# Attention, soft experts and feed-forward on one core: a fixed order for the feed-forward part, two more slots for weight loads, and longer rows in two kinds of loads

## The chip, the cores and the metric

The kernel runs on one core of one Trainium2 chip. The metric is the device time of one launch in microseconds (us). Three runs of the kernel before took 878.2, 876.0 and 877.66 us (median 877.66).

## What is computed

Three parts follow one another on 2304 tokens (4 batches of 576, 8 heads of 64):

```python
scores = scale * q @ k^T                              # per batch and head, 576x576
kth    = np.partition(scores, -32)[..., -32]          # keep the 32 largest of a row
attn   = softmax(where(scores >= kth, scores, -1e9)) @ v
x      = attn as [2304, 512]

logits = x @ phi                                      # [2304, 32]: 8 experts x 4 slots
slot_input = softmax(logits, axis=0).T @ x
slot_out[e] = relu(slot_input[e] @ w1[e]) @ w2[e]     # w1 512x1024, w2 1024x512
x      = softmax(logits, axis=1) @ slot_out           # the mix back to tokens

h      = x @ w_in                                     # 512x2048, float64
g      = where(h >= 1, h, where(h <= -1, 0, (h + 1)**2 / 4))
out    = g @ w_out                                    # 2048x512, float64
```

## The kernel before

**Attention** takes 16 head pairs through an order written by hand: the table `ORDER` names small operations, and each entry's letter says how many frames (one per pair) behind it runs. Among the entries are `c0` to `c6`: the conversion of one 128x512 tile of `w_in` from float64 to float32 by bit operations (`narrow`, L213 to L225: absolute value of the high word, maximum, low word scaled by 2^-51, shift by 3, integer add, sign, product with the sign), 16 tiles in all, stored to the DRAM tiles `cv_d` and loaded again later.

**Weight loads** all go through one queue on SP. `wload` (L135) takes the next entry of `worder`, a free 512 KB slot from `wfree`, and starts the transfer; a slot returns to `wfree` when the tile pool that owned it is done. The order is: `w1` (32 tiles), `w2` (32 tiles, w_32 to w_63), converted `w_in` and raw float64 `w_out` (16 tiles). `w2` and `cv_d` come in runs of 2 KB, `w_out` in runs of 4 KB.

**Experts.** For each of two groups of four experts: h = slot_input @ w1 (L804), so = relu(h) @ w2 (L823, four experts packed in row strips), a copy of it on ACT (L828) and a transpose (L831, copied by DVE at L835). Meanwhile `mix` turns the logits into the token-mix matrix `cT` (transposes L790 into one of the two PSUM buffers of the pool `ps_m`, copied out by ACT at L792). `m_first` (L841) multiplies slot_out with the first 512 columns of `w_in`; `m_rest` (L850) does the other 1536; `m_spread` (L865) unpacks one of them. So h of the feed-forward part is cT with m, and needs no 512-deep product.

**Feed-forward.** Tokens are cut into 6 blocks t of 384, the 2048 inner columns into 16 chunks f of 128: 96 steps (t, f). The list `steps` takes blocks 0 and 1 together, f by f (32 steps), then blocks 2 to 5 one after the other (64 steps). A step issues `emit_g` for the step two later: h (L898), two activations (L900, L901), then on DVE the clip (L902), a copy to the rounded high part gh (L904) and the rest gl (L905); then `emit_o` (L916): nine matmuls, 3 row tiles by gh·wh, gh·wl, gl·wh. In the first 32 steps each chunk of `w_out` is also made ready by `wo_prep`: the seven operations of `narrow`, on ACT (L213, L215, L217), POOL (L219 maximum, L223 integer add, L225 product with the sign) and DVE (L221 shift), then the high part wh on ACT (L891) and the low part wl on DVE (L892). In a step's name below, (t, f) is block and chunk.

In this part the order of the instructions on each engine is made by the scheduler, from the program order and its cost estimates. The last `NLAST` = 3 steps run row tile by row tile, so that each result row can be copied out (L920) and stored (L921).

Of the kernel before, what the change touches and what calls it, by code (L numbers as in the profile page):

```python
# [7 lines left out]
ET = mybir.EngineType  # L8
# [11 lines left out]
P = 128  # L20
# [20 lines left out]
NEG = -1.0e30  # L41
CW = 512
# [3 lines left out]
NRAW = 2  # L46
# [19 lines left out]
z3a H0b G31a S40a c0b T30b M21a c1b K11a L3a E40b T31b mc B0a P00a O21a mc c3b R3b C40a  # L66
# [7 lines left out]
def kernel_body(tc, qT, kT, vP, phi, w1, w2, w_in, w_out, out, fast, flag):  # L74
# [8 lines left out]
    cT = cpool.tile([P, NT], F32R, name="cT")  # L83
# [21 lines left out]
    cv_d = [p_dram.tile([P, CW], F32, name=f"cv_d{i}") for i in range(NCV)]  # L105
# [10 lines left out]
    worder += [(2, 0, 0), (2, 0, 1)] + [(3, 0, n) for n in range(NWE // 2)] + [(4, 0, NWE + n) for n in range(NRAW)] + [(2, 0, n) for n in range(2, 2 * NHP)]  # L116
# [14 lines left out]
    wfree = list(slots_a)  # L131
# [9 lines left out]
    def wload(n):  # L141
        while n > 0 and wfree and wnext[0] < len(worder):
            l, e, c = key = worder[wnext[0]]
            slot = next((x for x in wfree if l < 4 or len(x) == 1), None)
            if slot is None:
                return
            wfree.remove(slot)
            ring.append(slot)
            full, parts = slot_tiles(slot, f"w_{wnext[0]}", I32 if l == 4 else F32)
            if l == 0:  # L150
                src = w1[e, c * P:(c + 1) * P, :].rearrange("p (n f) -> p n f", n=2)
            elif l == 1:
                src = w2[e, c * 2 * P:(c + 1) * 2 * P, :].rearrange("(n p) f -> p n f", p=P)
            elif l == 4:
                src = w_out[c * P:(c + 1) * P, :].bitcast(I32).rearrange("p (n f) -> p n f", n=2)
            else:
                src = None
            if full is not None and src is not None:
                dmas = [(full, src)]
            elif src is not None:  # L160
                dmas = [(parts[m], src[:, m, :]) for m in range(2)]
            else:
                n0, c0 = divmod(c, 2)
                at = [NC1 * (2 * c0 + m) + n0 if l == 2 else NHP * NC1 + 2 * c + m for m in range(2)]
                dmas = [(parts[m], cv_d[at[m]]) for m in range(2)]
# [482 lines left out]
    def emit(name, pi):  # L648
        k = name[0]
        if k == "l":  # L650
            op_late(pi, name[1])
        elif k == "z":
            op_split(pi + 1, int(name[1]))
        elif k == "m":
            if pi % NHP == NHP - 1:
                op_moe(pi, k)
        elif k in "cd":
            if k == "c" or pi < NWE:
                i = pi + min(pi, NWE) + (k == "d")
                if i < NCV:  # L660
                    conv_op(i, int(name[1]))
        else:
# [51 lines left out]
    wfree.extend(cv_slots + half_slots)  # L714
# [41 lines left out]

    def mix():
        wide = [P, NR + 1, B, NSLOT]
# [20 lines left out]
        for b in range(B):  # L779
# [6 lines left out]
            for rows in (range(NR), (NR,)):  # L786
# [5 lines left out]
                nc.scalar.copy(cT[:, b * S + rows[0] * P:b * S + rows[0] * P + w],  # L792
# [6 lines left out]
    for g in range(2):  # L799
# [46 lines left out]
    def m_rest():  # L846
# [7 lines left out]
        for n in range(1, NC1):  # L854
            rows = slice(32 * n, 32 * n + 32)
# [27 lines left out]
    def wo_prep(f):  # L883
        if f < NWE:
            wo = wtile[(3, 0, f // 2)][f % 2]
        else:
            tr = p_t.tile([P, 2, CW], I32, name="tr_l", tag="h1s", bufs=2)
            sg = p_t.tile([P, CW], BF16, name="sg_l", tag="sg_l", bufs=1)
            wo = narrow(wtile[(4, 0, f)], tr, sg, range(7))
        wh, wl = slot_tiles(w_slots[f], "whl", F32R)[1]  # L890
        nc.scalar.copy(wh, wo)  # L891
        nc.vector.tensor_tensor(wl, wo, wh.bitcast(F32), op=ALU.subtract)  # L892
        wo_t[f] = (wh, wl)

    def emit_g(s_):
# [27 lines left out]
    m_first()  # L923
    for k in range(CLA):
        wo_prep(k)
    for s_ in steps[:GA]:
        emit_g(s_)
    for i, s_ in enumerate(steps[:-NLAST]):
        t, f = s_
        if i == 1:  # L930
            mhl = m_rest()
        if t == 1 and f % 4 == 1 and f // 4 < NC1 - 1:
            m_spread(f // 4 + 1, *mhl)
        if t == 0 and f + CLA < NF:
            wo_prep(f + CLA)
        if i + GA < len(steps):
            emit_g(steps[i + GA])
        emit_o(t, f, range(NS))
    for s_ in steps[GA - NLAST:] if NLAST > GA else []:
        emit_g(s_)  # L940
    for n in range(NS):
        for s_ in steps[-NLAST:]:
            emit_o(*s_, [n])
# [65 lines left out]
```

## Time and profile before

| | us |
|---|---|
| median of three runs | 877.66 |
| span of the profiled execution | 872.0 |
| its TensorE busy time | 821.5 (94%) |
| its VectorE / ScalarE / GpSimd busy time | 685.8 / 644.8 / 485.4 |
| last expert matmuls end, first o matmuls start | 614.71, 634.20 |
| last o matmul of the blocks 0 and 1, last of all | about 720, 865 |

The page gives the busy time of each engine, the busy tenths in 40 slices of 21.8 us, and the chain of work that ended last. Line numbers are those of the kernel before unless the text says otherwise. The profiled execution's span, 872.0 us, is 5.7 us below the median of the runs, which also hold what lies around the span; sums are made in the span's time and then moved by that 5.7 us.

### The profile page before, as it was taken

The page shows a single profiled execution, that of the slowest core. Times are in us where ns is not written, and L with a number is a line of the kernel's source. Part 1 is how long each engine was busy: PE and PEld are TensorE (multiplying, and loading weights), DVE is VectorE, ACT ScalarE, POOL GpSimd, SP SyncE. Part 2 cuts the span into 40 slices and gives each one's busy share as a digit, 9 for nine tenths or more (in the row PEclk, how much of TensorE's full clock was granted, in tenths as well). Part 3 has the DMA queues.
Part 4 walks back from the last instruction along what each step waited for, and adds up shares of the span by engine and source line. Part 5 has one row for each costly group of instructions (what it writes and reads, how often), then busy time and mean ns, then how long its engine had stood idle before and what let it go on. Part 6 is the DMA issues. An engine that isn't in the chain of part 4 may idle for free.

```text
span 872.0 us, 17711 instructions
## 1 busy us (share of the span) xinstructions
PE 821.5 (94%) x5695; PEld 674.7 (77%) x5695; DVE 685.8 (79%) x3084; ACT 644.8 (74%) x1292; POOL 485.4 (56%) x494
## 2 busy tenths in 40 slices
PE   4889999999999999999999999799698899999996
PEld 3678989988989988988988988632266678888885
DVE  6999999988999989999989994103389995666663
ACT  5688999988998988998988987412578766545453
POOL 2577888877888877888877774100467740000000
PEclk9799999999999999999999999899799999999999
DMA  8453563553353353353452536699940001001001
GB/s 240 124 152 96 165 176 98 156 157 89 103 142 92 112 133 89 102 142 87 117 134 78 157 101 205 206 343 386 399 175 1 0 2 73 37 0 38 1 37 40
DMA packets 49461, 108.59 MB, mean 125 GB/s; under 512 B 8304, under 2 KB 8304, under 8 KB 49360
## 3 DMA queue, kind: packets, MB, share of 16 engines
q1 hardware_dynamic: 49040, 106.73, 40.2%
q8 instruction: 47, 0.77, 0.4%
q10 hardware_dynamic: 320, 0.66, 0.3%
q14 instruction: 54, 0.44, 0.2%
HBM read 70.70 MB, written 8.91 MB: 91 GB/s over the span
## 4 chain that ended last, share of the span: by engine, by line
PE 78%; DVE 10%; DMA 6%; ACT 3%; POOL 1%; issue 1%; ACTq 0%; POOLq 0%; SPq 0%; DVEq 0%
PE s_ps L311 20%; PE o_ps L916 17%; PE av_ps L485 14%; PE pt_ps L457 7%; PE s_ps L413 4%; PE av_ps L486 3%; PE rem_ps L230 3%; DMA w<-in_moe_w_dram 2%; DMA w<-in_moe_w_out_dram 2%; PE h L804 2%; DVE cand L338 2%; PE moe_ps L569 2%; DMA w<-cv_d 1%; PE h_ps L898 1%; PE xT_ps L534 1%
## 5 line engine op out<-in xcount | busy, mean ns | idle before, releaser
L311 PE MATMUL s_ps<-kh,q 128*128 128x288 f32 x640 | 208.1, 342 | 16.4 <-DVE q L266 9.0
L916 PE MATMUL o_ps<-whl,ghl 128*128 128x512 f32 x864 | 216.9, 395 | 5.0 <-DVE ghl L904 4.0
L916 PEld LDWEIGHTS o_ps<-whl,ghl 128*128 128x128 f32 x864 | 159.1, 188 | 44.7 <-DVE ghl L904 7.1
L445 POOL TENSOR_TENSOR ssb<-ssb,pen 128x576 f32<-128x576 f32 x141 | 180.4, 1284 | 18.3 <-ACT pen L442 15.8
L311 PE MATMUL s_ps<-kl,q 128*128 128x288 f32 x640 | 181.2, 299 | 0.0
L338 DVE MAX8 cand<-ssb 128x8 f32<-128x82 f32 (+1 forms) x1008 | 164.2, 228 | 5.0 <-ACT ssb L329 4.0
L311 PEld LDWEIGHTS s_ps<-kh,q 128*128 128x128 f32 x640 | 123.6, 193 | 34.7 <-DVE q L266 9.4
L485 PE MATMUL av_ps<-v_sb,ptb 128*128 128x65 f32 (+1 forms) x1280 | 147.1, 261 | 0.4 <-ACT xT L547 0.4
L485 PEld LDWEIGHTS av_ps<-v_sb,ptb 128*128 128x128 f32 (+1 forms) x1280 | 141.1, 181 | 5.2 <-issue 2.6
L311 PEld LDWEIGHTS s_ps<-kl,q 128*128 128x128 f32 x640 | 124.4, 194 | 0.3
L422 DVE MAX8 l<-s_ps 128x8 f32<-128x576 f32 x144 | 109.2, 758 | 18.3 <-PE s_ps L413 17.9
L442 ACT ACTIVATE pen<-ssb,kb 128x576 bf16<-128x576 f32 x141 | 110.3, 792 | 4.5 <-POOL kb L438 3.3
L329 ACT COPY ssb<-s_ps 128x576 f32<-128x576 f32 x144 | 91.1, 641 | 25.3 <-PE s_ps L311 21.8
L448 ACT ACTIVATE ssb<-ssb,nm 128x576 f32<-128x576 f32 x141 | 109.0, 785 | 0.6 <-POOL ssb L445 0.6
L900 ACT ACTIVATE rg<-h_ps,half 128x384 f32<-128x384 f32 x96 | 55.2, 579 | 71.0 <-PE h_ps L898 70.8
L396 POOL TENSOR_SCALAR mb<-ssb,top 128x576 bf16<-128x576 f32 x48 | 83.3, 1736 | 19.2 <-DVE top L345 9.2
L902 DVE SCALAR_TENSOR_TENSOR rg<-h_ps,rg 128x384 f32<-128x384 f32 x96 | 52.9, 554 | 47.4 <-ACT rg L901 47.1
L467 ACT COPY ptb<-pt_ps 128x512 f32<-128x512 f32 x144 | 82.4, 598 | 3.3 <-PE av_ps L485 3.3
L457 PE MATMUL pt_ps<-ident,ssb 128*128 128x128 f32 x576 | 84.3, 273 | 0.2
L398 DVE TENSOR_SCALAR_CACHE_REDUCE mb<-ssb,top 128x576 bf16<-128x576 f32 x96 | 75.8, 802 | 0.0
L345 DVE MAX8 top<-cand 128x8 f32<-128x56 f32 x432 | 73.5, 207 | 0.1
L457 PEld LDWEIGHTS pt_ps<-ident,ssb 128*128 128x128 f32 x576 | 68.7, 142 | 1.3 <-ACT ptb L467 0.8
(160 smaller groups left out, 1311.7 us busy)
## 6 DMA issues: line engine op xcount, KB each, us to landing
w<-in_moe_w_dram SPq DMA_DIRECT2D x60, 512.0 KB, 6.7
q<-qst SPq DMA_DIRECT2D x60, 160.0 KB, 3.1
kh<-kst SPq DMA_DIRECT2D x60, 144.0 KB, 2.5
kl<-kst SPq DMA_DIRECT2D x60, 144.0 KB, 2.9
x<-in_moe_w_in_dram SPq DMA_DIRECT2D x16, 512.0 KB, 3.9
w<-in_moe_w_out_dram SPq DMA_DIRECT2D x16, 512.0 KB, 9.3
v_sb<-in_v_dram SPq DMA_DIRECT2D x16, 325.0 KB, 2.9
raw_t<-in_q_dram SPq DMA_DIRECT2D x15, 320.0 KB, 3.7
```

Source lines behind the costliest of these rows:

```text
L311: nc.tensor.matmul(s[:, hf, :HS], a, w, start=(n == 0), stop=(n == len(terms) - 1), skip_group_check=True)
L329: nc.scalar.copy(st[u]["ssb"][:, j], st.pop((u, j))[:, :, :HS])
L338: nc.vector.max(st[u]["cand"][:, j, 8 * g:8 * g + 8], row(u, j)[:, S * g // NSEG:S * (g + 1) // NSEG])
L396: nc.gpsimd.tensor_scalar(st[u]["mb"][:, j], row(u, j), t_u, None, op0=ALU.is_ge)
L422: nc.vector.max(st[u]["l8"][:, j], st.pop((u, j))[:, :, :HS])
L442: nc.scalar.activation(pen, row(u, j), AF.Relu, bias=st[u]["kb"][:, j:j + 1], scale=-BIG)
L445: nc.gpsimd.tensor_tensor(row(u, j), row(u, j), st.pop((u, "pen", j)), op=ALU.subtract)
L448: nc.scalar.activation(row(u, j), row(u, j), AF.Exp, bias=st[u]["nm"][:, j:j + 1], scale=0.125)
L457: nc.tensor.transpose(pt[:, c, :], pr[:, c * P:(c + 1) * P], ident)
L467: nc.scalar.copy(ptb, st.pop((u, "pt", j)))
L485: nc.tensor.matmul(o, pj[:, c, sl], v_sb[:, 4 * jj + c, :], start=(c == 0), stop=False)
L916: nc.tensor.matmul(pos[t][n], a[:, sl], w, start=(f == 0 and k == 0), stop=(f == NF - 1 and k == 2))
```

## The change

1. **Feed-forward part.** The scheduler no longer orders it: it is issued in program order on PE, ACT, DVE and POOL. `wo_prep` is split into the stages of `prep(f, k)`, spread over steps: stage 0 and 1 of chunk f+4 in step (1, f), stage 2 of chunk f+3 and stages 3 and 4 of chunk f+2 in step (0, f). The sign is put in by one DVE operation on bits (`scalar_tensor_tensor`, L911 after) instead of ACT's sign and POOL's product. The low part wl (L915 after) moves from DVE to POOL, except for the first two chunks. The copy gh moves from DVE to ACT (L932 after) for block 1, chunks 1 to 12. `emit_g` is cut into `emit_h` (h, two activations, clip) and `emit_g` (gh, gl). `m_rest` runs ahead of step (1, 1) instead of ahead of the second step, `m_spread` one f later.
2. **Loads.** The token-mix matrix `cT` is allocated only when `mix` runs, as two halves; until then these two slots carry weight tiles. So two more tiles (w_34 and w_35) are loaded before the queue's wait at the end of attention; their number `NRAW` of raw `w_out` tiles ahead of the rest of the converted weights goes from 2 to 4.
3. **Conversion one frame ahead.** `c4`, `c2`, `c5`, `c6` go from frame c to b, `c0`, `c1`, `c3` from b to a; the conversion's slots go to weight loads behind its last operation rather than behind the attention part.
4. **Runs of 4 KB.** A `w2` tile is loaded with two neighbouring rows of 512 in a partition (the columns of h1 are taken in the matching order when it is transposed), and two `cv_d` tiles lie side by side in one DRAM tile, so that a tile comes in runs of 4 KB. Where a slot consists of two halves, runs stay at 2 KB.

```diff
-NRAW = 2
+NRAW = 4
-cT = cpool.tile([P, NT], F32R, name="cT")
+p_ct = ctx.enter_context(tc.tile_pool(name="p_ct", bufs=1))
-cv_d = [p_dram.tile([P, CW], F32, name=f"cv_d{i}") for i in range(NCV)]
+cv_d = [p_dram.tile([P, 2, CW], F32, name=f"cv_d{i}") for i in range(NCV // 2)]
...
-    wfree = list(slots_a)
+    loan = [whole(p_ct, f"cT{n}", 1) for n in range(2)]
+    wfree = loan + slots_a
...
-                src = w2[e, c * 2 * P:(c + 1) * 2 * P, :].rearrange("(n p) f -> p n f", p=P)
+                src = w2[e, c * 2 * P:(c + 1) * 2 * P, :].rearrange("(p n) f -> p n f", n=2)
...
-        for n in range(1, NC1):
-            rows = slice(32 * n, 32 * n + 32)
+        for rows in (slice(32, 64), slice(64, P)):
             nc.scalar.copy(mh[rows], ps[rows])
...
+    def prep(f, k, last=None):
+        x64 = wtile[(4, 0, f)]
+        hf = x64[:, :, 1].bitcast(F32)
...
+        t, r = preps[f][:, 0], preps[f][:, 1]
+        tf = t.bitcast(F32)
+        if k == 0:
+            nc.scalar.activation(tf, hf, AF.Abs)
+            nc.gpsimd.tensor_scalar(tf, tf, 2.0 ** -15, None, op0=ALU.max)
+        elif k == 1:
+            nc.scalar.activation(r.bitcast(F32), x64[:, :, 0].bitcast(U32), AF.Identity, bias=two, scale=2.0 ** -51)
+        elif k == 2:
+            nc.vector.tensor_scalar(t, t, 3, None, op0=ALU.logical_shift_left)
+            nc.gpsimd.tensor_tensor(t, t, r, op=ALU.add)
+        elif k == 3:
+            nc.vector.scalar_tensor_tensor(t, x64[:, :, 1], SIGN, t, op0=ALU.bitwise_and, op1=ALU.bitwise_or)
+        else:
+            wh, wl = wo_t[f] = slot_tiles(w_slots[f], "whl", F32R)[1]
+            nc.scalar.copy(wh, tf)
+            (last or nc.gpsimd).tensor_tensor(wl, tf, wh.bitcast(F32), op=ALU.subtract)
...
+    def emit_g(s_, on_act=False):
+        g = gs.pop(s_)
         gh, gl = (x[:, :BLK] for x in ring_tile("g", g_slots, "ghl", F32R))
-        nc.vector.tensor_copy(gh, g)
+        if on_act:
+            nc.scalar.copy(gh, g)
+        else:
+            nc.vector.tensor_copy(gh, g)
         nc.vector.tensor_tensor(gl, g, gh.bitcast(F32), op=ALU.subtract)
...
+    def step(i):
+        t, f = steps[i]
+        nxt = steps[i + GA] if i + GA < len(steps) else None
+        if i == 3:
+            mhl.extend(m_rest())
+        if t == 1 and f % 4 == 2 and f // 4 < NC1 - 1:
+            m_spread(f // 4 + 1, *mhl)
+        if t == 0:
+            prep(f + 2, 3)
+        if nxt:
+            emit_h(nxt)
+        if t == 0:
+            prep(f + 2, 4)
+            prep(f + 3, 2)
+        elif t == 1:
+            prep(f + 4, 0)
+        if nxt:
+            emit_g(nxt, t == 1 and f + 4 < NF)
+        if t == 1:
+            prep(f + 4, 1)
         emit_o(t, f, range(NS))
...
+    with tc.manual_schedule(engines={ET.PE, ET.Activation, ET.DVE, ET.Pool}):
...
+        m_first()
+        emit_h(steps[0])
+        prep(0, 3)
+        prep(0, 4, nc.vector)
+        prep(1, 2)
+        emit_g(steps[0])
+        prep(2, 0)
+        prep(2, 1)
+        emit_h(steps[1])
+        emit_g(steps[1])
+        prep(1, 3)
+        prep(1, 4, nc.vector)
...
+        for i in range(len(steps) - NLAST):
+            step(i)
```

How the order moves, at three places. First PE between the last expert matmuls and `m_first`. Before (c_ps is a transpose of the mix, so an expert product, soT its transpose, m_ps the product with `w_in`):

```order
L790 MATMUL c_ps<-ident,c_9721 128x128 x4
L790 MATMUL c_ps<-ident,c_9721 128x64
L823 MATMUL so_9745<-w_9461,h1T_9619 32x512
L790 MATMUL c_ps<-ident,c_9733 128x128 x4
L790 MATMUL c_ps<-ident,c_9733 128x64
L823 MATMUL so_9745<-w_9463,h1T_9619 32x512
...
L823 MATMUL so_9745<-w_9467,h1T_9619 32x512
L831 MATMUL soT_ps<-ident,so_sb 128x128 x4
L841 MATMUL m_ps_9789<-w_9469,so_9531 128x512 x2
```

After:

```order
L829 MATMUL so_9737<-w_9459,h1T_9609 32x512
L829 MATMUL so_9737<-w_9461,h1T_9609 32x512
L795 MATMUL c_ps<-ident,c_9713 128x128 x4
L795 MATMUL c_ps<-ident,c_9713 128x64
L795 MATMUL c_ps<-ident,c_9725 128x128 x4
L795 MATMUL c_ps<-ident,c_9725 128x64
L837 MATMUL soT_ps<-ident,so_sb 128x128 x4
L847 MATMUL m_ps_9793<-w_9463,so_9521 128x512 x2
```

The last two mix transposes stood among the last expert matmuls; they now stand between these and the transpose soT.

Second, DVE in the steady part of the first 32 steps. Before, in two f (two steps with a conversion between them):

```order
L892 TENSOR_TENSOR whl<-tr_l,whl 128x512
L221 TENSOR_SCALAR tr_l<-tr_l 128x512
L902 SCALAR_TENSOR_TENSOR rg<-h_ps,rg 128x384
L904 CAST ghl<-rg 128x384
L905 TENSOR_TENSOR ghl<-rg,ghl 128x384
L902 SCALAR_TENSOR_TENSOR rg<-h_ps,rg 128x384
L904 CAST ghl<-rg 128x384
L905 TENSOR_TENSOR ghl<-rg,ghl 128x384
```

After:

```order
L911 SCALAR_TENSOR_TENSOR tr_l<-w_9501,tr_l 128x512
L925 SCALAR_TENSOR_TENSOR rg<-h_ps,rg 128x384
L908 TENSOR_SCALAR tr_l<-tr_l 128x512
L934 CAST ghl<-rg 128x384
L935 TENSOR_TENSOR ghl<-rg,ghl 128x384
L925 SCALAR_TENSOR_TENSOR rg<-h_ps,rg 128x384
L935 TENSOR_TENSOR ghl<-rg,ghl 128x384
```

One subtraction (wl, L892) and one of two copies gh have left DVE, and the bit operation L911 has come; the shift L908 now stands between a step's clip and its gh.

Third, POOL in the same steps. Before:

```order
L219 TENSOR_SCALAR tr_l<-tr_l 128x512
L223 TENSOR_TENSOR tr_l<-tr_l 128x512
L225 TENSOR_TENSOR tr_l<-tr_l,sg_l 128x512
```

After:

```order
L904 TENSOR_SCALAR tr_l<-tr_l 128x512
L915 TENSOR_TENSOR whl<-tr_l,whl 128x512
L909 TENSOR_TENSOR tr_l<-tr_l 128x512
```

POOL still has three operations for a chunk: the product with the sign is gone, and the subtraction wl stands ahead of the add of the next chunk.

## Rows read from the trace of the kernel before

**Rows 1.** The page, parts 1 and 2: busy time of the engines, then the granted TensorE clock and the DMA share in 40 slices of 21.8 us (tenths).

```profile
PE 821.5 (94%) x5695; PEld 674.7 (77%) x5695; DVE 685.8 (79%) x3084; ACT 644.8 (74%) x1292; POOL 485.4 (56%) x494
...
PEclk9799999999999999999999999899799999999999
DMA  8453563553353353353452536699940001001001
```

**Rows 2.** The chain that ended last, in order of time, from the end of attention to the first o matmuls: start, length, what it consisted of.

```profile
565.11 2.40 PE moe_ps L618 x48
...
588.92 10.78 DMA w<-in_moe_w_dram
599.77 10.87 DMA w<-in_moe_w_dram
610.65 7.28 DMA w<-cv_d
618.00 5.36 DMA w<-cv_d
623.42 8.37 DMA w<-in_moe_w_out_dram
631.85 8.55 DMA w<-in_moe_w_out_dram
```

**Rows 3.** What SP's DMA queue waited for: us in total, times, longest. L167 is the load of a weight tile.

```profile
SPq L167 <- PE moe_ps L618: 6.6, 1, 6.6
```

**Rows 4.** Three stretches: busy time of each engine, then granted clock, DMA share and GB/s. The first loads w2 (2 KB runs), the last raw w_out (4 KB runs).

```profile
590.00:600.00 10.00, 10.00 (x72) 3.54 (x73) 1.71 (x6) 1.44 (x3) 0.00 (x0) 1.00 1.05 387
...
624.00:632.00 8.00, 4.64 (x16) 1.25 (x19) 3.48 (x7) 5.79 (x11) 3.38 (x4) 0.50 1.03 409
632.00:640.00 8.00, 7.30 (x32) 3.98 (x26) 4.78 (x8) 5.47 (x10) 4.04 (x4) 0.91 1.03 410
```

**Rows 5.** PE in order of time: start, busy time, line, what, count, idle time before and what ended it. The row at 715.36 begins with step (1, 14), that at 637.19 is step (0, 1), that at 634.20 step (0, 0).

```profile
612.00 0.86 PE L790 MATMUL c_ps<-ident,c 128*128 128x128 f32 x5
612.79 1.92 PE L823 MATMUL so<-w,h1T 128*32 128x512 f32 x14
615.40 0.66 PE L831 MATMUL soT_ps<-ident,so_sb 128*128 128x128 f32 x4 [0.69 <-ACT so_sb L828]
616.77 3.70 PE L841 MATMUL m_ps<-w,so 128*128 128x512 f32 x8 [0.71 <-DVE so L835]
...
627.98 6.29 PE L850 MATMUL m_ps<-w,so 128*32 128x512 f32 x24
634.20 2.33 PE L916 MATMUL o_ps<-whl,ghl 128*128 128x512 f32 x9
...
637.19 2.32 PE L916 MATMUL o_ps<-whl,ghl 128*128 128x512 f32 x9 [0.44 <-DVE ghl L904]
...
715.36 4.34 PE L916 MATMUL o_ps<-whl,ghl 128*128 128x512 f32 x18
...
858.72 6.46 PE L916 MATMUL o_ps<-whl,ghl 128*128 128x512 f32 x27
```

**Rows 6.** ACT in order of time, around the last expert matmuls and at the end of the kernel, and SP's queue at its end.

```profile
612.70 0.70 ACT L792 CAST cT<-c_ps 128x512 fp32r<-128x512 f32 x2 [1.07 <-PE c_ps L790]
614.76 0.58 ACT L828 COPY so_sb<-so 128x512 f32<-128x512 f32 x1 [1.37 <-PE so L823]
...
864.75 1.56 ACT L920 COPY o_sb<-o_ps 128x512 f32<-128x512 f32 x3 [4.69 <-PE o_ps L916]
...
865.36 1.32 SPq L921 DMA_DIRECT2D out_dram<-o_sb  x3
```

**Rows 7.** ACT and DVE groups from 640 to 712 us (busy time, mean ns of one), and one POOL group of the attention part (a subtraction of two f32 tiles of 576 columns).

```profile
L900 ACT ACTIVATE rg<-h_ps,half 128x384 f32<-128x384 f32 x27 | 15.4, 572 | 7.1 <-PE h_ps L898 6.9
L901 ACT ACTIVATE rg<-rg 128x384 f32<-128x384 f32 x27 | 13.9, 519 | 0.3
...
L215 ACT ACTIVATE tr_l<-w,two 128x512 f32<-128x512 uint32 x12 | 9.0, 753 | 0.0
...
L891 ACT CAST whl<-tr_l 128x512 fp32r<-128x512 f32 x12 | 7.4, 616 | 1.4 <-POOL tr_l L225 1.3
...
L284 POOL TENSOR_TENSOR kst<-raw_t,kst 128x576 fp32r<-128x576 f32 x15 | 21.2, 1411 | 0.0
```

**Rows 8.** DVE and then POOL in order of time, around 703 to 709 us.

```profile
704.35 0.87 DVE L904 CAST ghl<-rg 128x384 fp32r<-128x384 f32 x1
705.26 1.40 DVE L905 TENSOR_TENSOR ghl<-rg,ghl 128x384 fp32r<-128x384 f32 x1
706.59 0.55 DVE L902 SCALAR_TENSOR_TENSOR rg<-h_ps,rg 128x384 f32<-128x384 f32 x1
707.23 0.36 DVE L904 CAST ghl<-rg 128x384 fp32r<-128x384 f32 x1
707.51 0.69 DVE L892 TENSOR_TENSOR whl<-tr_l,whl 128x512 fp32r<-128x512 f32 x1
...
708.58 0.42 DVE L221 TENSOR_SCALAR tr_l<-tr_l 128x512 int32<-128x512 int32 x1
...
703.40 1.61 POOL L223 TENSOR_TENSOR tr_l<-tr_l 128x512 int32<-128x512 int32 x1 [0.61 <-DVE tr_l L221]
705.09 1.16 POOL L225 TENSOR_TENSOR tr_l<-tr_l,sg_l 128x512 f32<-128x512 f32 x1
```

More of the change, by code (lines that the diff above doesn't have):

```diff
@@ L41 @@
 NEG = -1.0e30
+SIGN = -2 ** 31
 CW = 512
@@ L115, in kernel_body @@
     worder = [(l, 4 * g + e, c) for l in range(2) for g in range(2) for c in range(4) for e in range(4)]
-    worder += [(2, 0, 0), (2, 0, 1)] + [(3, 0, n) for n in range(NWE // 2)] + [(4, 0, NWE + n) for n in range(NRAW)] + [(2, 0, n) for n in range(2, 2 * NHP)]
+    worder += [(2, 0, 0), (2, 0, 1)] + [(4, 0, NWE + n) for n in range(NRAW)] + [(2, 0, n) for n in range(2, 2 * NHP)]
     worder += [(4, 0, f) for f in range(NWE + NRAW, NF)]
@@ L147, in wload @@
             wfree.remove(slot)
-            ring.append(slot)
+            if slot not in loan:
+                ring.append(slot)
             full, parts = slot_tiles(slot, f"w_{wnext[0]}", I32 if l == 4 else F32)
@@ L156, in wload @@
             else:
-                src = None
-            if full is not None and src is not None:
+                src = cv_d[c]
+            if full is not None:
                 dmas = [(full, src)]
-            elif src is not None:
+            else:
                 dmas = [(parts[m], src[:, m, :]) for m in range(2)]
[L162 to L165, printed above, removed]
             for dst, sr in dmas:
@@ L713, in kernel_body @@
                     emit(name, frame - k)
[L714 removed]
+    wfree.extend(half_slots)
     wload(99)
@@ L755, in mix_tile @@
         return t.rearrange(f"p ({' '.join(axes)}) -> p {' '.join(axes)}", **dict(zip(axes, shape[1:])))
+    cT = []
     def mix():
+        cT.extend(p_ct.tile([P, NT // 2], F32R, name=f"cT{n}", tag=f"cT{n}", bufs=1) for n in range(2))
         wide = [P, NR + 1, B, NSLOT]
@@ L791, in mix @@
                 w = len(rows) * n
-                nc.scalar.copy(cT[:, b * S + rows[0] * P:b * S + rows[0] * P + w],
+                nc.scalar.copy(cT[b // 2][:, b % 2 * S + rows[0] * P:b % 2 * S + rows[0] * P + w],
                                ps.rearrange("p a b -> p (a b)")[:, :w])
@@ L881, in kernel_body, with emit_h @@
     wo_t = {}
-    def wo_prep(f):
-        if f < NWE:
-            wo = wtile[(3, 0, f // 2)][f % 2]
-        else:
[L887 to L895, printed above, removed]
+    preps = {}
+    def prep(f, k, last=None):
+        if f >= NF:
+            return
+        x64 = wtile[(4, 0, f)]
+        hf = x64[:, :, 1].bitcast(F32)
+        if k == 0:
+            if f % 3 == 2:
+                preps[f] = slot_tiles(mix_slots[0], "tr_l", I32)[0]
+            else:
+                preps[f] = p_t.tile([P, 2, CW], I32, name="tr_l", tag="h1s", bufs=2)
+        t, r = preps[f][:, 0], preps[f][:, 1]
+        tf = t.bitcast(F32)
+        if k == 0:
+            nc.scalar.activation(tf, hf, AF.Abs)
[7 more added lines that the diff above has]
+            nc.vector.scalar_tensor_tensor(t, x64[:, :, 1], SIGN, t, op0=ALU.bitwise_and, op1=ALU.bitwise_or)
+        else:
+            wh, wl = wo_t[f] = slot_tiles(w_slots[f], "whl", F32R)[1]
+            nc.scalar.copy(wh, tf)
+            (last or nc.gpsimd).tensor_tensor(wl, tf, wh.bitcast(F32), op=ALU.subtract)
+            del preps[f]
+    def emit_h(s_):
         t, f = s_
         ph = ps_m.tile([P, 512], F32, name="h_ps", tag="m_ps")[:, :BLK]
-        nc.tensor.matmul(ph, m4[f // 4][:, f % 4 * P:(f % 4 + 1) * P], cT[:, t * BLK:(t + 1) * BLK], start=True, stop=True)
+        nc.tensor.matmul(ph, m4[f // 4][:, f % 4 * P:(f % 4 + 1) * P], cT[t // 3][:, t % 3 * BLK:(t % 3 + 1) * BLK], start=True, stop=True)
         r, g = (x[:, :BLK] for x in ring_tile("g", g_slots, "rg", F32))
@@ L921, in emit_o @@
                 nc.sync.dma_start(out[t * BLK + n * P:t * BLK + (n + 1) * P, :], o)
[L923 to L932, printed above, removed]
-            m_spread(f // 4 + 1, *mhl)
[L934 to L937, printed above, removed]
-        emit_o(t, f, range(NS))
[L939 to L943, printed above, removed]
+    def step(i):
[4 more added lines that the diff above has]
+        if t == 1 and f % 4 == 2 and f // 4 < NC1 - 1:
+            m_spread(f // 4 + 1, *mhl)
+        if t == 0:
[11 more added lines that the diff above has]
+            prep(f + 4, 1)
+        emit_o(t, f, range(NS))
+    mhl = []
+    with tc.manual_schedule(engines={ET.PE, ET.Activation, ET.DVE, ET.Pool}):
+        prep(0, 0)
+        prep(0, 1)
+        prep(0, 2)
+        prep(1, 0)
+        prep(1, 1)
+        m_first()
[10 more added lines that the diff above has]
+        prep(1, 4, nc.vector)
+        prep(2, 2)
+        prep(3, 0)
+        prep(3, 1)
+        for i in range(len(steps) - NLAST):
+            step(i)
+        for s_ in steps[GA - NLAST:]:
+            emit_h(s_)
+            emit_g(s_)
+        for n in range(NS):
+            for s_ in steps[-NLAST:]:
+                emit_o(*s_, [n])
     tail.close()
```

22 lines of the change are left out of this document (14 added, 8 removed).

## The prediction, made before the changed kernel was run

> **What bounds it now.** I read four views in this order. The page first: PE is busy for 821.5 of 872.0 us, so only stretches in which PE has little to do, or runs at a low clock, can give much. The slices show one such place, the 27th to 30th (567 to 654 us), where the DMA share is at 9 and the granted clock dips [rows 1]. Then the chain that ended last: from 588.92 to 640.40 us every piece is a weight transfer [rows 2]. Each hop spans eight 512 KB tiles, so a tile takes about 1.35 us in the w2 part (10.87 / 8). SP had stood for 6.6 us behind the last attention products before it could load more [rows 3]; they end at 565.11 + 2.40 = 567.5, and from there the loads run without a gap. Third, PE in order of time: the last expert matmuls end at 614.71, `m_first` starts at 616.77, step (0, 0) at 634.20, step (0, 1) at 637.19, step (1, 14) at 715.36, the last of all ends at 858.72 + 6.46 = 865.18 [rows 5]. So three stretches follow: loads until `m_first`; a start-up of 17.4 us; 28 steps from (0, 1) to (1, 14) in 78.2 us, 2.79 each; 67 steps in 149.8 us, 2.236 each. The last is PE's own pace, so a pair of steps (one f) costs PE 4.47 us, while the pairs with a conversion take 5.59. Fourth, DVE and POOL beside each other, to see why. A copy gh takes 0.36 us alone, but 0.87 when it is issued at 704.35 while POOL's add of two tiles runs (703.40 to 705.01): it ends 0.21 behind POOL's end. POOL's next two-tile operation starts at 705.09, ahead of the gl that DVE issues at 705.26, and gl takes 1.40 and ends 0.41 behind POOL [rows 8]. So in these rows a two-tile operation on POOL and a copy or two-tile operation on DVE exclude each other, and POOL's next operation may enter before DVE's.
>
> **1. Loads.** Two more tiles are loaded before the 6.6 us wait, so 28 rather than 30 tiles of w2 follow it. And with 4 KB runs they should move as `w_out` does, at 410 rather than 387 GB/s [rows 4]: 524,288 B in 1.279 rather than 1.355 us. Gain until the last w2 tile: 2 × 1.355 + 28 × 0.076 = 4.8 us. Bounds: 2.7 if the run length does nothing, 4.8 if it does all. I take 4.7, since the two rates come from the same queue 30 us apart.
> The Trainium skill (DMA: Bandwidth & Descriptors, section "Where 436 GB/s comes from") says that for transfers between HBM and SBUF the HBM side binds, at about 358 GB/s for a core. By it the run length is no lever and the gain would be 2.7, `m_first` 2.1 later than I have it. The trace speaks against it, with 387 and 410 GB/s in two stretches of one execution.
>
> **2. Between the expert matmuls and `m_first`.** Before, the last mix transposes ran among the last expert matmuls (612.00, ahead of the last 14), and the copy of `so` on ACT followed 0.05 us behind the matmuls' end [rows 5, 6]. Now two transposes stand between the last expert matmul and soT. Both need a PSUM buffer that ACT's cT copies free, and these stand in ACT's queue around the so copy. Of the 4.7 us I take off 1.1: one transpose of 0.86 [rows 5] and a part of a 0.70 copy [rows 6] that the so copy used to cover. So `m_first` starts at 616.77 − 3.6 = 613.2. Bounds: 612.0 (nothing lost) to 616.8 (all lost, if the mix chain is late). **−3.6.**
>
> **3. Start-up.** With fixed order, step (0, 0) no longer waits behind three later chunks. Walked from the rows: `m_first` 3.7, two copies of m 1.3, h 0.2, L900 0.57, L901 0.52, clip 0.55, bit operation about 0.69 (it has no row; the nearest is the subtraction of the same size at 707.51, and the lower bound a one-operand 0.42), wh 0.62, wl 0.69, gh and a gl held up by POOL's add 1.8: 11 us, so 624.2. But `m_rest` is now behind three steps, and DVE goes on in order: clip of (1, 0), gh, gl, bit operation, wh, wl of chunk 1 (to 628.0), shift, POOL's add, chunk 2's bit operation, its wl on POOL (to 632.5), shift, gh, POOL's add, gl. Step (0, 1) cannot start before about 634.2: 21.0 us after `m_first`, against 20.4 before. **+0.6.** What starts early here comes to nothing, since only two steps get through. `m_rest` took 6.29 us at a granted clock of 0.50 [rows 4, 5]; PE idles around it again, so up to 3 us more is possible.
>
> **4. The pairs with a conversion.** This is the term that decides. DVE's fixed order in a pair is bit operation, clip, shift, gh, gl, clip, gl; POOL's is maximum, wl, add; ACT copies gh of block 1. A walk round the ring, from the clip of a (1, f) to the next: clip 0.55; gh on ACT 0.52 (as L901, the same size); L215 0.75 and L900 0.57, which stand behind it on ACT; L901 0.52; clip of the next (0, f) 0.55; shift 0.42 [rows 7, 8]. That is 3.9. By then ACT's wh copy is done, and wl waits on POOL only for the shift to end. wl is a subtraction of two f32 tiles: POOL took 1.41 for 576 columns [rows 7], so 1.25 for 512. It enters ahead of gh, as POOL did ahead of DVE at 705.09. gh ends 0.2 behind it; but the add, which needs only the shift, stands right behind wl and enters ahead of gl, again as at 705.09: 1.3 more, and gl ends 0.4 behind that. Sum 3.9 + 1.25 + 1.25 + 0.4 = 6.8, less 0.1 for operations that overlap their predecessor's end: **6.7 us for a pair**, where PE needs 4.47.
> From (0, 1) to (1, 14) there are thirteen pairs and one step: one of 8.6 with `m_rest`, six of 6.7, five of about 6.1 (the three pairs with `m_spread`, which delays h, and a follower of it each, where wl goes first and the add alone collides), one without conversion 4.5, one step 2.2: 86.0 us, against 78.2. So (1, 14) starts at 613.2 + 21.0 + 86.0 = 720.2 rather than 715.36. **+7.8** in the pairs. Bounds: PE's own pace, 27 × 2.236 + 3.5 for `m_rest` and `m_spread` = 63.9, and 6.8 for every pair plus `m_rest`, 93.
> What leaves DVE (wl 0.69 and one gh 0.36 a pair) and ACT (the sign) is no gain, since neither engine was full: what bounds is the order in which they wait for each other.
>
> **5. The rest.** The 67 last steps run at PE's pace in both, DVE and ACT far ahead: 0. Before the end, `emit_g` of the last step is issued behind the first of the last three steps' products, which may bare some of its chain: +0.5. At the end three row copies came together (1.56 us on ACT) with three stores (1.32 us on SP) [rows 6]; in fixed order two of them lie beside matmuls: −1.0 (one copy and one store remain).
>
> **6. Conversion one frame ahead.** No instruction is added. Its stores and loads move past other loads of SP's queue by a frame; the work beside it leaves PE little idle time, 6% over the whole span [rows 1], and the moved operations are the same 16 × 7. 0; bounds −1 and +2, the latter if POOL's three operations fall on a thresholding that is waited for.
>
> **Sum.** −3.6 + 0.6 + 7.8 + 0.5 − 1.0 = +4.3: span 876.3. The median of the runs lies 5.7 above the span shown, so **882 us**.
>
> **Rivals.**
> A (forecast): POOL enters ahead of gh and gl in most pairs. 882, by itself 878 to 887 (`m_first` 1.2 earlier or, as in C, 3.6 later). Chance 0.45.
> B: POOL gets in once a pair, gl or gh before it at other times, so pairs keep the pace of before, 5.59. 27 steps at 2.79 = 75.4 rather than 86.0: 871.5. For it: the mix of cheap (0.36) and dear (0.87) copies that the rows show. 0.20.
> C: `m_first` is no earlier, because the mix transposes wait for ACT and PSUM: 3.6 later than A, 886. It decides if the second-to-last cT copy ends later than the last expert matmul by over 4 us. Against it: the mix's transposes ran 2 us before the end as soon as DVE gave them c. 0.08.
> D: DVE holds gh and gl together and wl lands in the gap while ACT works: pairs at PE's pace, 882 − 22 = 860. Against it: wl's only wait, the wh copy, ends before the shift. 0.12.
> E: collisions in every second pair, 6.2 a pair (13 × 0.5 us less, less the pairs that were 6.1 already: about −4): 878, no change. 0.15.
> Slower ones are A and C, faster ones B and D; about what three runs can tell from no change is 0.3%, 2.6 us, 875.0 to 880.3. A reaches a little into it, E a little out. Faster 0.33, same 0.17, slower 0.50. The range that holds the time 8 times in 10 takes A, B and E whole and half of D: 860 to 887.
>
> **What the profile after would show.** If right: the last expert matmuls end near 609, `m_first` starts near 613; step (0, 0) near 624 but (0, 1) near 634; steps (0, f) then come 6 to 7 us apart, with idle time of PE in each pair ended by DVE's gl; DVE's gh and gl rows of block 0 are longer than 1.2 us, and start while POOL's wl or add runs; (1, 14) starts near 720; from there all is as before. If B or D: gh rows near 0.4 us, pairs of 5.6 or 4.5. If C: idle PE between the last so product and soT of over 4 us. What would make the forecast wrong is above all the order in which POOL and DVE get in, since 10 of the us hang on it, and after that the bit operation's time, once in each pair.

## The result and the profile after

The changed kernel takes 888.0 us (median of four runs, 884.9 to 888.8), the kernel before 876.8 (four runs): a ratio of 1.0107, with an interval of 1.0069 to 1.0145. It is slower, as forecast, but by 9.4 us on that ratio (11.2 between the medians) where the sum said 4.3, and the 888.0 lies just above the range's upper end of 887. The profiled execution has a span of 886.6 us.

PE of the changed kernel in order of time, at the places of [rows 5] (start, busy time, line, what, idle time before and what ended it):

```profile
608.43 0.83 PE L795 MATMUL c_ps<-ident,c 128*128 128x128 f32 x5 [2.52 <-DVE c L789]
...
614.29 0.86 PE L795 MATMUL c_ps<-ident,c 128*128 128x128 f32 x5
615.62 0.86 PE L795 MATMUL c_ps<-ident,c 128*128 128x128 f32 x5 [0.47 <-ACT cT L797]
616.96 0.66 PE L837 MATMUL soT_ps<-ident,so_sb 128*128 128x128 f32 x4 [0.47 <-ACT cT L797]
618.37 3.67 PE L847 MATMUL m_ps<-w,so 128*128 128x512 f32 x8 [0.76 <-ACT tr_l L906]
...
628.38 1.19 PE L946 MATMUL o_ps<-whl,ghl 128*128 128x512 f32 x2 [2.23 <-DVE ghl L934]
...
638.51 0.71 PE L946 MATMUL o_ps<-whl,ghl 128*128 128x512 f32 x2 [1.40 <-ACT tr_l L903]
...
643.24 3.64 PE L856 MATMUL m_ps<-w,so 128*32 128x512 f32 x24
...
729.13 2.26 PE L946 MATMUL o_ps<-whl,ghl 128*128 128x512 f32 x9
...
875.20 5.28 PE L946 MATMUL o_ps<-whl,ghl 128*128 128x512 f32 x21 [0.89 <-DVE ghl L934]
```

`m_first` starts at 618.37, not at 613.2. Ahead of it stand the two mix transposes that the order had moved there (614.29 and 615.62), and each next PE step waits 0.47 us for ACT's cT copy. Step (0, 0) comes at 628.38 and (0, 1) at 638.51, 20.1 us after `m_first` (21.0 forecast). Step (1, 14) comes at 729.13, 90.6 us after (0, 1) (86.0 forecast). The last row shows a new wait: 0.89 us for the gh of the last step.

For the same two stretches before, [rows 5] name the wrong step. `steps` runs (0, 0), (1, 0), (0, 1), and so on, nine matmuls each, so the row at 637.19 is step (1, 0). Step (0, 1) of the kernel before is the next one:

```profile
641.16 1.66 PE L916 MATMUL o_ps<-whl,ghl 128*128 128x512 f32 x6
```

So before, (0, 1) came 24.4 us after `m_first` (not 20.4), and (1, 14) came 715.36 - 641.16 = 74.2 us after (0, 1) (not 78.2), in 27 steps. The start-up became 4.3 us shorter and the pairs 16.4 us longer.

The steady part, DVE and then POOL of the changed kernel, to be held beside [rows 8]:

```profile
659.52 0.56 DVE L925 SCALAR_TENSOR_TENSOR rg<-h_ps,rg 128x384 f32<-128x384 f32 x1 [0.54 <-ACT rg L924]
659.99 0.42 DVE L908 TENSOR_SCALAR tr_l<-tr_l 128x512 int32<-128x512 int32 x1
660.32 1.44 DVE L934 CAST ghl<-rg 128x384 fp32r<-128x384 f32 x1
661.80 1.52 DVE L935 TENSOR_TENSOR ghl<-rg,ghl 128x384 fp32r<-128x384 f32 x1
663.24 0.54 DVE L925 SCALAR_TENSOR_TENSOR rg<-h_ps,rg 128x384 f32<-128x384 f32 x1
664.36 0.56 DVE L935 TENSOR_TENSOR ghl<-rg,ghl 128x384 fp32r<-128x384 f32 x1 [0.58 <-ACT ghl L932]
664.84 0.69 DVE L911 SCALAR_TENSOR_TENSOR tr_l<-w,tr_l 128x512 int32<-128x512 int32 x1
666.07 0.56 DVE L925 SCALAR_TENSOR_TENSOR rg<-h_ps,rg 128x384 f32<-128x384 f32 x1 [0.54 <-ACT rg L924]
...
660.08 1.47 POOL L915 TENSOR_TENSOR whl<-tr_l,whl 128x512 fp32r<-128x512 f32 x1 [1.96 <-ACT whl L914]
661.51 1.39 POOL L909 TENSOR_TENSOR tr_l<-tr_l 128x512 int32<-128x512 int32 x1
662.87 1.79 POOL L904 TENSOR_SCALAR tr_l<-tr_l 128x512 f32<-128x512 f32 x1
```

One round is 666.07 - 659.52 = 6.55 us, and the walk can be read off (gh takes 0.36 and gl 0.56 where POOL does not hold them up): the shift ends at 660.41, POOL's wl gets in ahead of gh, which takes 1.44 and ends 0.21 behind wl (661.55); the add gets in ahead of gl, which takes 1.52 and ends 0.42 behind the add (662.90). After that DVE waits for ACT twice (0.58, 0.54).

### The profile page after: what moved, and what is told of

The parts are those of the page before. It is cut to its first block, busy times and chain, and to the rows that moved or that the text cites. A ratio compares the mean times of both kernels' runs of the same rounds, so it can differ in the third digit from the quotient of the medians.

```text
span 886.6 us, 17714 instructions
## 1 busy us (share of the span) xinstructions
PE 829.6 (94%) x5695; PEld 681.1 (77%) x5695; DVE 693.1 (78%) x3073; ACT 643.1 (73%) x1287; POOL 486.9 (55%) x492
## 4 chain that ended last, share of the span: by engine, by line
PE 76%; DVE 10%; DMA 6%; ACT 4%; issue 2%; POOL 1%; ACTq 0%; SPq 0%; POOLq 0%; DVEq 0%
PE s_ps L310 20%; PE o_ps L946 17%; PE av_ps L484 14%; PE pt_ps L456 7%; PE s_ps L412 4%; PE av_ps L485 3%; DMA w<-in_moe_w_dram 3%; PE rem_ps L229 3%; DMA w<-cv_d 2%; DVE ghl L934 2%; DVE cand L337 2%; PE moe_ps L568 2%; PE h_ps L921 1%; DVE rg L925 1%; PE xT_ps L533 1%
## 5 line engine op out<-in xcount | busy, mean ns | idle before, releaser
L946 PE MATMUL o_ps<-whl,ghl 128*128 128x512 f32 x864 | 226.1, 405 | 15.3 <-DVE ghl L934 7.3
L946 PEld LDWEIGHTS o_ps<-whl,ghl 128*128 128x128 f32 x864 | 164.1, 194 | 56.8 <-DVE ghl L935 12.7
L935 DVE TENSOR_TENSOR ghl<-rg,ghl 128x384 fp32r<-128x384 f32 x96 | 68.1, 709 | 9.9 <-ACT ghl L932 7.0
## 6 DMA issues: line engine op xcount, KB each, us to landing
w<-in_moe_w_out_dram SPq DMA_DIRECT2D x16, 512.0 KB, 10.2
```

What stands on the lines that cost most here:

```text
L946: nc.tensor.matmul(pos[t][n], a[:, sl], w, start=(f == 0 and k == 0), stop=(f == NF - 1 and k == 2))
```

## The experiments

**The kernel before, profiled again.** No edit. The first profile's span, 872.0, is short for its median.

> The kernel before once more, for a second profile. Theory (the profiled execution of before had a high granted clock in the expert part by chance, 0.983 over the span, and its h ended at 585.2, while four other kernels with the same code there end it at 587 to 590): from the first h matmul to m_first 49.5 to 51 us instead of 48.0, and 74 us again from the third feed-forward step to the one that starts at 715.36. Rival (the loads of the change make the expert part later): 48.0 again.

It took 877.9 us, span 875.7. Its `m_first`:

```profile
621.81 3.70 PE L841 MATMUL m_ps<-w,so 128*128 128x512 f32 x8 [0.71 <-DVE so L835]
```

From the first h matmul (569.79) that is 52.0 us, against 48.0 in [rows 5] (from 568.77). Granted clock (last but two), 570 to 575 us, in the first profile and in this one:

```profile
570.00:575.00 5.00, 5.00 (x52) 1.56 (x48) 0.00 (x0) 0.00 (x0) 0.00 (x0) 1.00 1.03 373
```

```profile
570.00:575.00 5.00, 5.00 (x28) 1.05 (x24) 0.14 (x1) 0.00 (x0) 0.00 (x0) 0.50 0.92 316
```

Same program, same work, but 52 matmuls at 1.00 there and 28 at 0.50 here. The first 90 h matmuls took 10.49 us there and 13.08 here, which is 2.6 of the 4.0 us; the other 1.4 lie behind the first transpose c_ps (605.88 there, 609.49 here), where the granted clock of 610 to 615 us was 1.00 there and 0.74 here. So the expert part of one profile is uncertain by some 4 us, all of it in stretches of another granted clock. In the changed kernel it took 49.6 (618.37 - 568.80), between the two, and its first 90 took 11.87. Both profiles of before agree on the rest: 98.6 and 97.2 us from `m_first` to step (1, 14) (74.2 of them from (0, 1) on in both), 149.4 and 149.5 from there to the start of the last matmul. The changed kernel has 110.8 and 151.0.

**Each half of the change alone.** The changed kernel's loads, slots and conversion with the feed-forward code of before:

```diff
 # on the changed kernel: from m_rest to the end of the loop over steps
-    def prep / emit_h / emit_g / step / manual_schedule ...
+    def wo_prep / emit_g / loop over steps          (before's text, cT in halves)
```

> The changed kernel with the feed-forward part of before (scheduler's order, wl and every gh on DVE, sign by ACT and POOL, m_rest ahead of the second step); loads, slots, 4 KB runs and conversion are the changed kernel's. Theory (the earlier loads are hidden behind the chain of the token mix, the loss is in the feed-forward part): m_first near 618, as in the changed kernel, no earlier than the 616.8 of before, and the time is that of before plus 0 to 2: 877 to 879. Rival (the loads gave their 3 to 5 us and the fixed order spoilt them): m_first near 613, 872 to 874. Rival (the loads part itself costs much of the 11 us): 882 or more.

888.7 us, ratio to before 1.0104 [1.0068, 1.0140]. The time is that of the last rival (882 or more), but the place is that of none: `m_first` stood at 620.4 (51.6 after the first h, within the 48.0 to 52.0 of before), so the loads neither gave nor took much there, and yet 10 us are gone. They go behind `m_first`, where the scheduler made another order (that other load times made it do so was not tried):

```profile
628.55 1.92 PE L857 MATMUL m_ps<-w,so 128*32 128x512 f32 x4
630.40 5.15 PE L923 MATMUL o_ps<-whl,ghl 128*128 128x512 f32 x18
...
635.66 3.62 PE L857 MATMUL m_ps<-w,so 128*32 128x512 f32 x20
...
652.33 7.91 PE L923 MATMUL o_ps<-whl,ghl 128*128 128x512 f32 x26 [0.43 <-DVE ghl L911]
```

`m_rest` is cut in two with two steps between, and the fourth step starts only at 652.33. From `m_first` to the ninth step it takes 48.7 us against 40.6 and 39.3 in the two profiles of before; from there to (1, 14) 58.8 against 58.0. So this run does not give the price of the loads: taking the fixed order away also lets the order change.

The other half, the new feed-forward part on the loads of before:

```diff
 # on the kernel before: m_rest to the end, from the changed kernel, cT undivided
+    def prep / emit_h / emit_g / step / manual_schedule ...
-NRAW = 4, loan, 4 KB runs, conversion a frame earlier     (not taken over)
```

> The kernel before with the feed-forward part of the changed kernel alone (fixed order, wl on POOL, gh of block 1 on ACT, sign by a bit operation, m_rest later); loads, runs and conversion are before's. Theory (the feed-forward part loses the time): m_first near 616.8, pairs with a conversion 6.5 us, about 886 (884 to 888). Rival (the later transposes of the mix and the loads cost the time): 878 to 880.

887.6 us, ratio 1.0102 [1.0075, 1.0129]: this half alone is enough for the whole loss, as the theory said. It lies where the theory puts it: from `m_first` to step (1, 14) it takes 108.1 us, against 98.6 and 97.2 before, and a pair takes 6.56 (clips at 677.44 and 684.00), with gh 1.44 and gl 1.53. `m_first` itself stood at 622.0 rather than near 616.8, since the first h started late, at 571.98; from there it is 50.1 us.

**The shift behind gh and gl.** One call moves behind another in step (0, f):

```diff
             prep(f + 2, 4)
-            prep(f + 3, 2)
...
             emit_g(nxt, t == 1 and f + 4 < NF)
+        if t == 0:
+            prep(f + 3, 2)
```

> The changed kernel with one exchange of places: the shift (and with it POOL's add) of the next chunk comes behind gh and gl of block 0 instead of ahead of them. Theory (POOL's two-tile operations enter ahead of gh and gl and DVE waits): gh is still held by wl, 1.4 us, but gl is short, 0.55; a pair 5.8 instead of 6.55 us, so 12 pairs give 8 us: 880 (878 to 883). Rival (the order on ACT, gh of block 1 ahead of the low-word conversion and the next step's activations, sets the pair): pairs stay at 6.5, 887 to 888.

879.0 us, 9 us less than the changed kernel; not told apart from before (ratio 1.0007 [0.9989, 1.0025]). DVE and POOL there:

```profile
657.38 0.36 DVE L934 CAST ghl<-rg 128x384 fp32r<-128x384 f32 x1
657.78 1.54 DVE L935 TENSOR_TENSOR ghl<-rg,ghl 128x384 fp32r<-128x384 f32 x1
659.25 0.41 DVE L908 TENSOR_SCALAR tr_l<-tr_l 128x512 int32<-128x512 int32 x1
...
663.05 0.36 DVE L934 CAST ghl<-rg 128x384 fp32r<-128x384 f32 x1
...
657.53 1.38 POOL L915 TENSOR_TENSOR whl<-tr_l,whl 128x512 fp32r<-128x512 f32 x1 [0.41 <-ACT whl L914]
```

A pair is 5.67 us (5.8 expected). It is gl that wl holds up, not gh as I expected; only one of the two is.

**The same with wl on DVE.**

```diff
-            prep(f + 2, 4)
+            prep(f + 2, 4, nc.vector)
```

> As the run before, and wl on DVE ahead of gh for every chunk, so that POOL has only the maximum and the add. Theory (POOL and DVE exclude each other): gh 0.36, gl 0.55, a pair 5.3 to 5.5 us: 13 us less than the changed kernel, 875 (873 to 878). Rival (the order on ACT): pairs 6.5 or longer, since DVE has 0.7 more to do in its chain: 888.

873.2 us, ratio to before 0.9933 [0.9904, 0.9962], faster than before.

```profile
679.34 0.35 DVE L934 CAST ghl<-rg 128x384 fp32r<-128x384 f32 x1
679.73 0.56 DVE L935 TENSOR_TENSOR ghl<-rg,ghl 128x384 fp32r<-128x384 f32 x1
...
682.41 1.09 DVE L911 SCALAR_TENSOR_TENSOR tr_l<-w,tr_l 128x512 int32<-128x512 int32 x1
...
684.80 0.35 DVE L934 CAST ghl<-rg 128x384 fp32r<-128x384 f32 x1
```

gh 0.35, gl 0.56, a pair 5.46: the waits for POOL in front of gh and gl are gone, and ACT's order has not changed. So it was not ACT's order that set 6.55.

**wl on DVE alone**, in the order of the changed kernel:

```diff
-            (last or nc.gpsimd).tensor_tensor(wl, tf, wh.bitcast(F32), op=ALU.subtract)
+            nc.vector.tensor_tensor(wl, tf, wh.bitcast(F32), op=ALU.subtract)
```

> The changed kernel with one edit: wl on DVE for all chunks; the shift stays ahead of gh. Theory (what costs is that a two-tile operation of POOL stands right in front of gh and gl; the add still does): DVE has wl 0.6 more in its chain, POOL's wl 1.4 less, gh is held by the add alone and gl is free, so a pair 5.9 to 6.3 instead of 6.55: 881 to 886. Rival (moving wl to POOL is what costs): 5.3 to 5.5 a pair, 874.

884.2 us, and a pair 6.12. POOL's add alone now stands in front of gl:

```profile
679.44 0.35 DVE L934 CAST ghl<-rg 128x384 fp32r<-128x384 f32 x1
679.83 1.56 DVE L935 TENSOR_TENSOR ghl<-rg,ghl 128x384 fp32r<-128x384 f32 x1
...
679.67 1.30 POOL L909 TENSOR_TENSOR tr_l<-tr_l 128x512 int32<-128x512 int32 x1 [3.08 <-ACT rg L923]
```

Moving wl to POOL costs 0.4 us a pair in this order; the place of the add costs more (6.12 to 5.46).

**The bit operation in the gap**, on the run with 873.2:

```diff
-        if t == 0:
-            prep(f + 2, 3)
...
-            prep(f + 2, 4, nc.vector)
+        if t == 0 and f > 0:
+            prep(f + 1, 4, nc.vector)
         elif t == 1:
             prep(f + 4, 0)
+            prep(f + 2, 3)
```

> As the run with a late shift and wl on DVE (873.2), and the bit operation moved by half a pair, into the time in which DVE waits for ACT's copy gh of block 1; the copy and wl of that chunk follow in the next pair. Theory (what is left of a pair above PE's 4.47 is DVE's own order around POOL's add): a pair 4.9 to 5.1 instead of 5.46, 867 to 869. Rival (ACT's order sets the pair, 4.7 busy and its waits): 5.4, 873.

870.2 us (867 to 869 expected), ratio 0.9921 [0.9895, 0.9947]; a pair 5.15, a little above the bound I gave:

```profile
678.93 0.54 DVE L925 SCALAR_TENSOR_TENSOR rg<-h_ps,rg 128x384 f32<-128x384 f32 x1
...
681.65 1.62 DVE L911 SCALAR_TENSOR_TENSOR tr_l<-w,tr_l 128x512 int32<-128x512 int32 x1
683.19 0.96 DVE L935 TENSOR_TENSOR ghl<-rg,ghl 128x384 fp32r<-128x384 f32 x1
684.08 0.55 DVE L925 SCALAR_TENSOR_TENSOR rg<-h_ps,rg 128x384 f32<-128x384 f32 x1
...
681.42 1.30 POOL L909 TENSOR_TENSOR tr_l<-tr_l 128x512 int32<-128x512 int32 x1 [1.95 <-DVE tr_l L908]
```

DVE now has no idle time left in a pair; the add is paid in the bit operation (1.62 instead of 0.69), and the gl behind it is longer too (0.96 instead of 0.56).

**What the loads are worth.** The feed-forward part of that run on the loads of before:

> The feed-forward part of the run with the bit operation in the gap (870.2), on the kernel before: its loads, run lengths, slots and conversion frames. Theory (the loads gain nothing as long as the mix chain and the in-order expert products set m_first): 870 to 871. Rival (the earlier loads are worth the 3 to 4 us that the pair of runs with the early mix differed by): 873 to 875.

870.6 against 870.2 us (ratios to before 0.9932 [0.9906, 0.9958] and 0.9921): nothing to be seen, but the times alone leave some 3 us open either way. The profiles are closer, since in both the first 90 h matmuls took the same time. New loads, then old:

```profile
568.97 11.83 PE L809 MATMUL h<-w,siT 128*32 128x512 f32 x90
618.49 3.67 PE L847 MATMUL m_ps<-w,so 128*128 128x512 f32 x8 [0.75 <-ACT tr_l L906]
```

```profile
569.02 11.83 PE L805 MATMUL h<-w,siT 128*32 128x512 f32 x90
618.37 3.70 PE L842 MATMUL m_ps<-w,so 128*128 128x512 f32 x8 [0.71 <-DVE so L836]
```

From the first h to `m_first` it takes 49.5 us with the new loads and 49.4 with the old.

Then the mix issued ahead of the first group's products, on the run with 873.2, with the new loads and with the old:

```diff
-        if g == 1:
+        if g == 0:
             mix()
```

> As the run with a late shift and wl on DVE (873.2), with the token mix issued ahead of the first group's products with w2 instead of behind them. Theory (the chain of the mix sets m_first, and the last w2 tile at 608.7 has long landed): m_first 2 to 4 us earlier against the first h matmul, 870. Rival (what sets m_first is the last expert matmuls themselves): m_first where it was, 873.

> As the run with the mix early, but with the loads, run lengths, slots and conversion frames of the kernel before. Theory (the loads of the change land 3 to 5 us earlier, which shows only when the mix is out of the way): m_first 2 to 4 us later than in the run with the mix early, 872 to 874. Rival (the loads are hidden in both): the same time, 870.

875.9 and 879.5 us; ratios to before 0.9973 [0.9952, 0.9994] and 1.0025 [1.0003, 1.0046]. With the mix early the new loads are worth 3.6 us by these medians, as the theory said; the profiles place 1.5 of them (from the end of the first 90 h matmuls to `m_first` 37.9 us with the new loads, 39.4 with the old). But the run with the early mix is 2.7 slower than 873.2, where I expected 3 gained. `m_first` did not move: it stands 50.5 us behind the first h, 50.3 in the run with 873.2, as the rival said. All four mix transposes are done by 618.1, and what ends last are the expert products:

```profile
612.01 0.83 PE L795 MATMUL c_ps<-ident,c 128*128 128x128 f32 x5 [2.92 <-DVE c L789]
...
617.28 0.86 PE L795 MATMUL c_ps<-ident,c 128*128 128x128 f32 x5
618.07 1.90 PE L829 MATMUL so<-w,h1T 128*32 128x512 f32 x10
619.91 0.65 PE L837 MATMUL soT_ps<-ident,so_sb 128*128 128x128 f32 x4
621.24 0.65 PE L837 MATMUL soT_ps<-ident,so_sb 128*128 128x128 f32 x4 [0.68 <-ACT so_sb L834]
622.65 3.67 PE L847 MATMUL m_ps<-w,so 128*128 128x512 f32 x8 [0.76 <-PE soT_ps L837]
```

PE stood 2.92 us for DVE's c, and the products that follow in its queue stood with it; now both transposes of so stand at the end. What the profiled execution lost against the run with 873.2 (3.0 us of span) lies ahead of all this: its first h started at 572.18 instead of 569.08, with PE's instructions in the same order up to there, but at a granted clock of 0.50 instead of 1.00 from 554 to 562 us. So the 2.7 us are not shown to be a price of the early mix.

**gh of block 0 on ACT too, and the last step's h earlier**, on the run with 870.2:

```diff
-            emit_g(nxt, t == 1 and f + 4 < NF)
+            emit_g(nxt, t < 2 and f + 4 < NF)
...
+        if i == len(steps) - NLAST - 1:
+            for x in steps[GA - NLAST:]:
+                emit_h(x)
+                emit_g(x)
         emit_o(t, f, range(NS))
```

> The run with the bit operation in the gap (870.2), with two edits that lie apart in time. First gh of block 0 on ACT too, beside wl on DVE: DVE is full in that kernel (5.14 a pair) and ACT has 0.7 idle; theory 4.8 a pair, 3 to 4 us less; rival (ACT becomes the bound at 4.9 and waits for both clips): 5.1 or more, no gain. Second the last step's h and g are issued one step earlier: the 0.9 us in which PE waited for the last gh goes, and the last 32 steps take 71.1 us as before instead of 72.3: 1.2 less. Together 865 to 866.

868.8 us, ratio 0.9914 [0.9886, 0.9942]: the fastest version, though not clear of 870.2, and short of the 865 to 866 expected. A pair is 5.01 (clip to clip, 676.17 to 681.18), so moving one more copy gained 0.1, and from `m_first` to step (1, 14) nothing (90.7 us against 90.4). The rival has it: ACT now works through a pair almost without a pause. At the end the wait for the last gh is gone,

```profile
852.74 9.00 PE L946 MATMUL o_ps<-whl,ghl 128*128 128x512 f32 x36
```

and the last 32 steps take 71.5 us to the start of the last matmul, 0.8 less than with it (1.2 expected).

## Why the prediction was right, and where it was wrong

**The mechanism was right.** POOL's two-tile operations enter ahead of DVE's gh and gl, once each in a pair. A pair was forecast at 6.7 and measured at 6.55; putting the add behind gh and gl gave 9 us back, and taking wl off POOL as well 15. Of the rivals, B, D and E (POOL gets in less often, or not) are excluded by the DVE rows: in all six pairs from 653 to 690 us gh takes 1.43 to 1.47 and gl 1.51 to 1.54. The size was not right: +4.3 was said, and two terms missed in the same direction.

**The step that failed is the first, "−3.6" for the loads and `m_first`.** The transfers ran at 406 to 415 GB/s from 580 to 615 us, as the sum had it; but the last w2 tile was not what the last expert products waited for. It was issued at 598.5 and took 10.2 us to land, so it was there at 608.7; the last ten products started at 612.38 and ended at 614.36, where "near 609" was forecast. The last products stand in PE's queue among the transposes of the mix, and the mix's chain on DVE and ACT started with a transpose 2.6 us later than in the first profile of before (598.88 against 596.24), because 82 instead of 70 expert products stood ahead of it and the clock was lower (the first 90 h matmuls took 11.87 instead of 10.49). I had taken off 1.1 us for the two transposes; from the end of the products to `m_first` it came to 4.0 instead of 2.1 us, 1.9 lost. Rival C has the result, no earlier `m_first` and 886, but not the cause as I had worded it: the second-to-last cT copy ended 1.3 us behind the last product (615.69), not over 4. I had held C at 0.08 by the argument that the transposes ran as soon as DVE gave them c: true, and no argument on when DVE would. That the term is near 0, not −3.6, is shown by old and new loads in kernels otherwise alike: 49.4 and 49.5 us from the first h to `m_first` where the first 90 h matmuls took the same time, and equal times of the whole twice (870.6 and 870.2, 887.6 and 888.0).

**Start-up and pairs were measured from the wrong step before.** The 21.0 and 86.0 forecast for (0, 1) were set against 20.4 and 78.2, which belong to (1, 0). Against 24.4 and 74.2 the same forecast reads −3.4 and +11.8 instead of +0.6 and +7.8, and a pair of before takes 5.50 rather than 5.59. The total, +8.4, is not touched, because what one stretch lacked the other had too much. Measured were −4.3 and +16.4.

**Beside it lay the 5.7 us between span and median.** I took it for what lies around the span. The changed kernel shows 1.8 (888.37 − 886.6) and the second profile of before 2.2; the rest was an execution some 3.6 us shorter than its median, with a high clock in the expert part. Its 616.77 was no good yardstick for `m_first`.

**The pairs were mis-sized by 4.6 us** (90.6 instead of 86.0). 2.9 of that is the pair with `m_rest`, 11.5 instead of 8.6 (638.51 to 650.03): I had counted its matmuls but not that on ACT and DVE the copies of their result stand ahead of the next step's activations and clip (ACT's copies at 647.00 and 648.32, the activation at 648.93, DVE's clip at 650.10). The rest is spread over the other pairs.

**The end**: +1.5 in the last steps instead of +0.5 (the 0.89 wait, and 6.84 instead of 6.46 us of work for the last 27 products), and 6.5 instead of 7.2 us behind the last matmul's start, −0.7 where −1.0 was said. Against the second profile of before the sum closes: −1.0 (attention) −2.5 (to `m_first`, within the clock's spread) +13.5 (to (1, 14)) +1.5 −0.7 = +10.8, and the spans differ by 886.6 − 875.7 = 10.9.

**Conversion a frame earlier** at 0 is borne out as far as the h matmuls start at 568.8 in both first profiles, and at 568.97 with the new order of conversion and 569.02 with the old in the two runs above; over all runs their start varied from 568.7 to 572.2.

What stays open: why the scheduler's order on the new loads is as much slower as it is (only its place was shown); how much of the 3.6 us between old and new loads with an early mix is the loads; and why the granted clock fell at 554 us in some executions and not in others.

## What to carry to other kernels

When two engines cannot work at the same time on two-tile operations, what an instruction costs is set by its place: ask which instruction of the other engine becomes ready at the moment when the first engine's chain goes on, and put the foreign one where that chain waits for a third engine anyway. A load that lands earlier is worth nothing until the instruction that waits for it is next in its engine's queue; read the queue, not the landing. Before a term of a few us is taken from one profile, see how far that execution lies from its median; and count the steps before a row is given a step's name.

## What the runs showed of the hardware that was not expected

The granted clock of the same 5 us stretch of the same program was 1.00 in one execution and 0.50 in another (28 instead of 52 matmuls), after the same work. The runs of one kernel spread by 3 to 7 us, and the shorter ones show the higher mean clock (875.4 us at 0.983 and 880.3 at 0.973 in the run with 879.0). A bit operation of two int32 tiles on DVE took 0.69 us alone, 1.62 while POOL's add ran, and 1.09 when POOL's one-tile maximum began just ahead of it; beside the same maximum gl was of its usual length in the changed kernel (0.56 at 651.23, all of it inside the maximum of 650.72 to 652.21) and longer in the run with 870.2 (0.96 at 683.19, inside 682.69 to 684.62). What decides between the two was not tried.
